# Narrower unread matmuls at the start, and seven output stores issued in halves, in an attention and mixer kernel

## The chip, the cores and the metric

The kernel runs on one core of one Trainium2 chip. The metric is the device time of one execution in microseconds (us). It was measured in three runs: 286.3, 287.03 and 287.74, a median of 287.03 us. A profile of one further execution was taken; its span, from the first to the last instruction, is 285.6 us.

The core has a matmul engine (PE, with its weight loads listed apart as PEld), a vector engine (DVE), an activation engine (ACT), a general engine (POOL) and a sequencer for transfers (SP). Each runs its own list of instructions in order and waits on semaphores for the others. Transfers (DMAs) are issued by SP, by ACT or by POOL and run on 16 DMA engines.

## The reference

Causal attention in blocks of 64 over 8 batches, 8 heads, 576 positions and 64 elements a head, followed by a mixer: one product over the positions, with a residual, and one over the channels, with a residual.

```python
def _attn_ref(q, k, v):
    scores = scale * np.matmul(q, k.transpose(0, 1, 3, 2))
    mask = block_i >= block_j            # blocks of 64 positions
    scores = np.where(mask, scores, -1000000000.0)
    scores = scores - np.max(scores, axis=-1, keepdims=True)
    attn = np.exp(scores)
    attn = attn / (np.sum(attn, axis=-1, keepdims=True) + 1e-09)
    return np.matmul(attn, v)

def _moe_ref(x, w_tok1, w_tok2, w_ch1, w_ch2):
    xt = x.transpose(0, 2, 1)
    h = np.maximum(xt @ w_tok1, 0.0) @ w_tok2
    u = x + h.transpose(0, 2, 1)
    h2 = np.maximum(u @ w_ch1, 0.0) @ w_ch2
    return u + h2
```

The output is float32, 8 x 576 x 512.

## The kernel before

The program is written as a list of operations. Each has the engines that may run it, the operations it depends on, and a function `emit` that issues its instructions. The text `ORDER` names all operations in the order in which they are emitted, each with the engine that runs it and the PSUM banks that it takes; so the order on every engine is fixed by hand, and a change inside one `emit` leaves the order of the operations as it is.

The batches are worked one after another, and pieces of neighbouring batches are interleaved on PE. For a batch, q and k are loaded and transposed on DVE (L442); PE makes scores of 64-row blocks (L566), ACT takes the exponentials (L585 for batch 0, L772 for most of the others), PE multiplies by v (L616, L669), and DVE divides by the sums. Then the mixer follows: the product over positions (L807 and L902), a transpose of the result `u_sb` to `uT` on PE for the early batches (L989) and by a DMA of SP from batch 2 on (L969, and L979 for the last 64 positions of two batches together, `um_sb`), the first channel product (L1030, L1103, L1227) and the second (L1361). DVE folds the second product's parts into `o_sb` (L1407), and SP stores `o_sb` to HBM (L1450 for the first 512 positions, L1436 for the rest).

Two places matter here.

The first is the start. `raise_clock` issues matmuls whose results nobody reads: their operands are a tile of zeros, `zeros`, which lies in `wd_sb`, and their output goes to a PSUM bank that is handed back at once. One operation at the very start of PE issues `WARM` = 11 of them with 512 columns (L371). Then there are 110 operations of one matmul with 256 columns each (L378), of which `ORDER` takes 37: 13 directly behind the first block, and 24 in groups of one to nine between the score matmuls of batch 0, up to 17.4 us. Each matmul is issued with its own load of 128 x 128 weights. The first score matmul waits for a transpose of q that waits for a load.

The second is the store of the output at the end of `channel_down_fast`. `o_sb` is a ring of three buffers, each of 128 x 2 x 512 float32, and a batch takes two of them, `row` 0 and `row` 1. For batches 0 to 6 both tiles of a row are finished together (`joint`), so a row is stored by one transfer of 512 KB on SP. Batch 7 is done in two turns of one tile each, in smaller transfers. SP's list also holds the transposes and the first loads of k and q. A buffer of `o_sb` may be written again when its store has landed.

Of the kernel before, what the change touches and what calls it, by code (L numbers as in the profile page):

```python
# [182 lines left out]
def kernel(  # L183
# [11 lines left out]
    nc = tc.nc  # L195
# [15 lines left out]
    def ring(n, shape, dtype, name, pool=sb):  # L211
        return [pool.tile(shape, dtype, name=f"{name}{i}", uniquify=False) for i in range(n)]
# [35 lines left out]
    o_sb = ring(3, [128, 2, DM], FP32, "o_sb")  # L248
# [13 lines left out]
    zeros = wd_sb[:, 0, 0:2, :].rearrange("p c s -> p (c s)")  # L262
# [16 lines left out]
    WARM, KEEP = 11, 110  # L279
# [25 lines left out]
    def bank_of(note):  # L305
        if note["pool"] in EARLY:
            return mm[note["slot"]]
        if not late:
            held_banks[0].__exit__(None, None, None)
            held_banks[0] = tc.tile_pool(name="singles", bufs=1, space=bass.MemoryType.PSUM)  # L310
            late.extend(ring(4, [128, 512], FP32, "late", held_banks[0].__enter__()))
        return late[note["slot"]]
# [8 lines left out]
    def reads(key, op):  # L321
        readers.setdefault(key, []).append(op)
        return op
# [41 lines left out]
    def raise_clock():  # L365

        bank = {"covers": True}

        def emit(o, bank=bank):
            for _ in range(WARM):  # L370
                nc.tensor.matmul(out=bank_of(bank), lhsT=zeros[:, 0:128], rhs=zeros, start=True, stop=True)  # L371

        P.add("PE", WARM * 0.427, emit, pads["zeros"], -1e6, take=[(BANK, bank)], give=[bank], at=1.2)
        for n in range(KEEP):
            bank = {"covers": False}

            def emit(o, bank=bank):
                nc.tensor.matmul(  # L378
                    out=bank_of(bank)[:, 0:256], lhsT=zeros[:, 0:128], rhs=zeros[:, 0:256],
                    start=True, stop=True,  # L380
                )

            P.add(
                "PE", 0.11, emit, pads["zeros"], 1e6, take=[(BANK, bank)], give=[bank], at=5.0 + 0.12 * n, until=20.0,
                quick=True,
            )
# [930 lines left out]
    def channel_down_fast(b, g_done, wc2_ready, u_done, prio):  # L1317
# [4 lines left out]
        oi, si = [], []  # L1322
# [9 lines left out]
        for ts in ((0, 1),) if joint else ((0,), (1,)):  # L1332
            c0, nt = ts[0], len(ts)
# [5 lines left out]
            for n, (dst, x, y, op) in enumerate(  # L1339
                ((s1, a21, a22, ADD), (s2, s1, a11, SUB), (s4, a12, s2, SUB), (a21, a11, a21, SUB))  # L1340
            ):
                def emit(o, dst=dst, x=x, y=y, op=op):
                    nc.vector.tensor_tensor(out=dst, in0=x, in1=y, op=op)

                war = s_war[n] if n < 3 else []
                made.append(P.add(
                    "DVE", dve_cost(768 * nt, 2), emit, g_done + war + made[-1:], prio - 2 + 0.1 * c0 + 0.01 * n,
                ))
                reads(g_key(b), made[-1])
# [3 lines left out]
            def product(n, to, x, y, made=None, s=None, c0=c0, nt=nt, banks=banks, last=last):  # L1353
                bank, first = banks[to], n in (0, 1)

                def emit(o, n=n):
                    if n == 0:
                        cover(banks["c"])
                    for i in range(nt):
                        for kk in range(H6):  # L1360
                            nc.tensor.matmul(  # L1361
                                out=bank_of(bank)[:, 256 * i : 256 * i + 256],
                                lhsT=x[:, kk, 128 * i : 128 * i + 128], rhs=y[:, kk],
                                start=first and i == 0 and kk == 0, stop=kk == H6 - 1,
                                skip_group_check=not first or i > 0,
                            )

                op = last[to] = P.add(
                    "PE", mm_cost(256, H6 * nt), emit, g_done + wc2_ready + wd_ready + [last.get(to), made],
                    prio + 0.005 * c0 + 0.02 * n,  # L1370
                    take=[(SEED, banks["c"]), (BANK, bank)] if n == 0 else [(BANK, bank)] if first else (),
                )
                reads(g_key(b), op)
                if s is not None:
                    reads(("s", si[s]), op)
                return op

            def turn(row, col):
                bank = {"covers": True}

                def emit(o):
                    for i in range(4):
                        nc.tensor.matmul(
                            out=bank_of(bank)[:, 128 * i : 128 * i + 128],
                            lhsT=uT[0][:, 2 * row + i // 2, 2 * col + i % 2, :], rhs=ident,
                            start=i == 0, stop=True, skip_group_check=i > 0,
                        )

                op = P.add("PE", mm_cost(128, 4), emit, u_done, prio - 0.5, take=[(BANK, bank)])
                reads(("uT", 0), op)  # L1390

                def emit(o):
                    cast(
                        o, ut[:, 2 * row : 2 * row + 2, 256 * col : 256 * col + 256],
                        bank_of(bank).rearrange("p (t c) -> p t c", c=256),
                    )

                return P.add(EVAC, evac_cost(512), emit, [op], prio - 0.5, give=[bank])
# [47 lines left out]
            rows = out[b, 0:512, :].rearrange("(r t p) d -> r p t d", r=2, t=2)  # L1446
            pieces = [(0, 0, 2), (1, 0, 2)] if c0 == 0 else [(0, 0, 2), (1, 1, 2), (1, 0, 1)]
            for row, h0, h1 in pieces:
                def emit(o, row=row, cols=slice(256 * h0, 256 * h1), c0=c0, nt=nt):
                    (nc.scalar if o.engine == "ACT" else nc.sync).dma_start(  # L1450
                        out=rows[row][:, c0 : c0 + nt, cols], in_=o_sb[oi[row]][:, c0 : c0 + nt, cols]
                    )

                op = P.add(
                    ("SP", "ACT") if b == B - 1 else "SP", 0.5, emit, [folded[row, h] for h in range(h0, h1)], prio, xfer=4 * 0.086 * nt * (h1 - h0)
                )
                reads(("o", oi[row]), op)
# [102 lines left out]
```

## Time and profile before

| | |
|---|---|
| median of 3 runs | 287.03 us (286.3 to 287.74) |
| profiled execution: span | 285.6 us |
| profiled execution: time | not listed |
| PE busy | 273.9 us, 96% of the span |
| DVE busy | 239.2 us, 84% |
| ACT busy | 179.4 us, 63% |
| POOL busy | 72.6 us, 25% |
| transfers | 31.96 MB, 112 GB/s on average |
| stores of 512 KB (L1450, SP) | 14, 3.2 us median to landing |

The profile's page gives busy time and the number of instructions of each engine, transfer queues, the chain of work that ended last, and the costliest groups of instructions. Rows of the chain have start, length and what ran. Rows of the timeline have start, length, engine, line, operation, output and input, and a count; neighbours of one form are merged, so the start of such a row is that of its first instruction, and its length reaches to the end of its last. In square brackets stands the idle time before it and what ended that. Rows of waits have who waited for whom, the sum in us, how often, and the longest. Rows of windows have the stretch, its length, and the busy time of PE, PEld, DVE, ACT and POOL with the count of instructions in brackets, then the granted clock, the share of the DMA engines and GB/s. A row for one line has its count, the shortest, the median and the longest duration in ns, and the first and the last start. Rows of queues have the packets, MB and the share of the DMA engines' time; the queue of kind "instruction" carries program code.

### The profile page before, as it was taken

How to read it: one execution, taken by the hardware profiler on the slowest of the kernel's cores; microseconds unless marked ns; L12 is line 12 of the kernel's file. 1: busy time of each engine (PE TensorE's matmuls, PEld its weight loads, DVE VectorE, ACT ScalarE, POOL GpSimd, SP SyncE). 2: the span in 40 equal slices, each digit the busy share in tenths (PEclk: the TensorE clock that was granted, in tenths of full speed). 3: DMA queues.
4: the chain of work that ended last, by engine and by line, in shares of the span. 5: the costliest groups of instructions: out<-in, count | busy, mean ns of one | idle time of the engine just before them, and what ended most of it. 6: DMA issues, size and time to landing. Idle time of an engine off the chain costs nothing.

```text
span 285.6 us, 9485 instructions
## 1 busy us (share of the span) xinstructions
PE 273.9 (96%) x4047; PEld 200.5 (70%) x4068; DVE 239.2 (84%) x515; ACT 179.4 (63%) x331; POOL 72.6 (25%) x126
## 2 busy tenths in 40 slices
PE   7899999999997999999999999999999999999992
PEld 3467565599675788986877668744589876578882
DVE  3588769999888898999998979769896995689982
ACT  3798888945996856897879865364524745642100
POOL 8895861502540351063332210000000000000000
PEclk9999999999999999999999999999999999999998
DMA  7999999936979492999598595101056301200255
GB/s 170 168 164 195 200 193 200 182 50 145 97 109 103 75 154 54 174 184 168 68 116 136 79 175 50 75 0 21 0 108 122 142 0 73 76 2 2 98 156 188
DMA packets 64778, 31.96 MB, mean 112 GB/s; under 512 B 53088, under 2 KB 55776, under 8 KB 64736
## 3 DMA queue, kind: packets, MB, share of 16 engines
q0 software_dynamic: 44896, 17.49, 53.0%
q1 hardware_dynamic: 19408, 13.21, 20.3%
q8 instruction: 32, 0.52, 0.7%
q10 hardware_dynamic: 432, 0.66, 0.7%
q14 instruction: 10, 0.08, 0.1%
HBM read 35.85 MB, written 9.44 MB: 159 GB/s over the span
## 4 chain that ended last, share of the span: by engine, by line
PE 90%; ACT 4%; DMA 1%; issue 1%; POOL 1%; DVE 0%; POOLq 0%
PE late L1361 23%; PE mm L1103 8%; PE mm L1227 7%; PE mm L566 7%; PE mm L1361 7%; PE late L1227 6%; PE late L1103 6%; PE mm L616 5%; PE mm L807 3%; PE late L616 2%; ACT e_sb L585 2%; PE mm L902 2%; PE late L566 2%; PE late L1030 2%; PE mm L1030 2%; PE late L807 2%
## 5 line engine op out<-in xcount | busy, mean ns | idle before, releaser
L772 ACT ACTIVATE e_sb<-mm 128x512 bf16<-128x512 f32 x82 | 46.6, 607 | 12.7 <-PE late L566 9.0
L772 ACT ACTIVATE e_sb<-late 128x512 bf16<-128x512 f32 x86 | 48.5, 610 | 9.2 <-PE late L566 8.4
L442 DVE STREAM_TRANSPOSE qk_sb<-qk_sb 128x288 int32<-128x288 int32 (+1 forms) x65 | 41.7, 695 | 3.4 <-PE sc L566 1.4
L468 POOL DMA_DIRECT2D vals<-in_v_dram x45 | 36.9, 829 | 5.9 <-PE mm L616 2.4
L1361 PEld LDWEIGHTS <-gT 128*128 128x128 bf16 x336 | 32.0, 98 | 5.6 <-issue 0.4
L1361 PEld LDWEIGHTS <-sums 128*128 128x128 bf16 x324 | 31.3, 98 | 5.2 <-issue 0.4
L566 PEld LDWEIGHTS <-qk_sb 32*64 32x64 bf16 x1280 | 19.6, 104 | 14.4 <-issue 10.7
L566 PE MATMUL mm<-qk_sb 32*64 32x512 bf16 (+7 forms) x560 | 27.4, 289 | 0.4
L616 PEld LDWEIGHTS <-e_sb 128*128 128x128 bf16 x640 | 23.3, 97 | 6.2 <-issue 3.6
L566 PE MATMUL late<-qk_sb 32*64 32x512 bf16 (+7 forms) x560 | 26.4, 294 | 0.3 <-ACT e_sb L585 0.3
L1361 PE MATMUL late<-wd_sb,gT 128*128 128x256 bf16 x168 | 20.7, 273 | 0.0
L1361 PE MATMUL late<-wd_sb,sums 128*128 128x256 bf16 x168 | 20.6, 273 | 0.0
L1103 PEld LDWEIGHTS <-ws_sb 128*128 128x128 bf16 x192 | 18.2, 98 | 3.0 <-issue 0.9
L642 DVE TENSOR_TENSOR x_sb<-mm,rinv 128x256 bf16<-128x256 f32 x45 | 18.7, 422 | 1.3
L616 PE MATMUL mm<-vals,e_sb 128*128 128x65 bf16 x450 | 19.7, 193 | 0.0
L1407 DVE TENSOR_TENSOR o_sb<-late,u_sb 128x512 f32<-128x512 f32 x22 | 15.0, 685 | 3.6 <-PE late L1361 3.6
L1361 PE MATMUL late<-wc_sb,gT 128*128 128x256 bf16 x132 | 16.2, 273 | 0.1
L1103 PEld LDWEIGHTS <-wc_sb 128*128 128x128 bf16 x144 | 15.3, 114 | 1.4 <-issue 0.4
L1227 PEld LDWEIGHTS <-ws_sb 128*128 128x128 bf16 x96 | 9.3, 98 | 9.8 <-issue 0.2
L594 POOL COPY vals<-e_sb 128x256 bf16<-128x256 bf16 (+1 forms) x11 | 4.3, 394 | 39.4 <-ACT e_sb L772 39.2
L400 ACT COPY mm<-late 128x512 f32<-128x512 f32 (+1 forms) x16 | 9.2, 572 | 8.1 <-PE late L1227 5.3
L793 ACT ACTIVATE gT<-mm 128x512 bf16<-128x512 f32 x21 | 12.6, 619 | 1.9 <-PE mm L1103 0.9
(198 smaller groups left out, 625.7 us busy)
## 6 DMA issues: line engine op xcount, KB each, us to landing
out_dram<-o_sb SPq DMA_DIRECT2D x14, 512.0 KB, 3.2
qk_sb<-in_k_dram POOLq DMA_DIRECT2D x14, 288.0 KB, 6.3
qk_sb<-in_q_dram POOLq DMA_DIRECT2D x14, 288.0 KB, 5.8
vals<-in_v_dram POOLq DMA_DIRECT2D x28, 128.0 KB, 4.5
wc_sb<-in_moe_w_ch_dram POOLq DMA_DIRECT2D x8, 192.0 KB, 7.7
wc_sb<-in_moe_w_ch_dram POOLq DMA_DIRECT2D x3, 512.0 KB, 10.4
out_dram<-o_sb SPq DMA_DIRECT2D x5, 256.0 KB, 3.3
vals<-in_v_dram POOLq DMA_DIRECT2D x15, 64.0 KB, 5.1
```

The lines of the kernel that those rows point to most:

```text
L442: nc.vector.transpose(dst[:, 0:S, :] .rearrange("p s e -> p (s e)") .bitcast(I32) .rearrange("p (a k) -> p k a", k=NB)[:, k0:k1], raw2.bit ...
L468: nc.gpsimd.dma_start(out=t[128 - p : 128, J, hs, 0:64], in_=src)
L566: nc.tensor.matmul(out=home(n)[64 * half : 64 * half + 64, c : c + w], lhsT=bar[r, 0] if j is None else kT[i][r, 64 * j : 64 * j + 64, par ...
L616: nc.tensor.matmul(out=u[:, I, 0:65], lhsT=e[:, h, c : c + 128], rhs=vt[:, J, head, 0:65], start=(J == 0), stop=(J == I),)
L642: nc.vector.tensor_tensor(out=xt[:, 0:4, 64 * head : 64 * head + 64], in0=u[:, :, 0:64], in1=ri[:, 0:4].to_broadcast([128, 4, 64]), op=MULT,)
L772: nc.scalar.activation(dst, bank_of(x), EXP, scale=scale)
L793: nc.scalar.activation(dst, src, RELU)
L807: nc.tensor.matmul(out=ps, lhsT=w1_sb[:, c, tt : tt + 255 : 2], rhs=xt[:, c, cols], start=(c == 0), stop=False)
L1103: nc.tensor.matmul(out=bank_of(bank)[:, 256 * o_ : 256 * o_ + 256], lhsT=x(o_, m), rhs=y[:, :, m, :], start=opens, stop=m == 1, skip_group ...
L1227: nc.tensor.matmul(out=bank_of(bank), lhsT=x(m), rhs=y[:, :, m, :], start=first and m == 0, stop=m == 1, skip_group_check=not first,)
L1361: nc.tensor.matmul(out=bank_of(bank)[:, 256 * i : 256 * i + 256], lhsT=x[:, kk, 128 * i : 128 * i + 128], rhs=y[:, kk], start=first and i ...
L1407: nc.vector.tensor_tensor(out=dst, in0=src, in1=other, op=ADD)
```

## The change

`raise_clock` issues 40 matmuls of 128 columns and one of 512 in place of 11 of 512: 5,632 columns in both. Each matmul of 256 columns (L378) becomes two of 128 in the same bank. The store of `row` 0 in batches 0 to 6 becomes two transfers, one for each tile of 128 rows; `row` 1 is stored as before. In batch 7 `nt` is 1, so nothing changes there, and the stores of the last 64 positions (L1436) are untouched.

PE's program grows by 134 instructions (67 loads and 67 matmuls, all of them up to 17.4 us in the old timeline), SP's by seven transfers. DVE, ACT and POOL have the same operations in the same order. The semaphores that SP's and ACT's transfers take in turn (eight of them) are dealt out anew behind the first split store, and where an operation waits for a store of a whole row 0 it now waits for two transfers.

```diff
         def emit(o, bank=bank):
-            for _ in range(WARM):
-                nc.tensor.matmul(out=bank_of(bank), lhsT=zeros[:, 0:128], rhs=zeros, start=True, stop=True)
+            for n in range(4 * WARM - 3):
+                w = 128 if n < 4 * WARM - 4 else 512
+                nc.tensor.matmul(
+                    out=bank_of(bank)[:, 0:w], lhsT=zeros[:, 0:128], rhs=zeros[:, 0:w], start=True, stop=True,
+                )
...
             def emit(o, bank=bank):
-                nc.tensor.matmul(
-                    out=bank_of(bank)[:, 0:256], lhsT=zeros[:, 0:128], rhs=zeros[:, 0:256],
-                    start=True, stop=True,
-                )
+                for i in range(2):
+                    nc.tensor.matmul(
+                        out=bank_of(bank)[:, 128 * i : 128 * i + 128], lhsT=zeros[:, 0:128], rhs=zeros[:, 0:128],
+                        start=True, stop=True,
+                    )
...
                 def emit(o, row=row, cols=slice(256 * h0, 256 * h1), c0=c0, nt=nt):
-                    (nc.scalar if o.engine == "ACT" else nc.sync).dma_start(
-                        out=rows[row][:, c0 : c0 + nt, cols], in_=o_sb[oi[row]][:, c0 : c0 + nt, cols]
-                    )
+                    step = 1 if row == 0 else nt
+                    for t0 in range(c0, c0 + nt, step):
+                        (nc.scalar if o.engine == "ACT" else nc.sync).dma_start(
+                            out=rows[row][:, t0 : t0 + step, cols], in_=o_sb[oi[row]][:, t0 : t0 + step, cols]
+                        )
```

## The prediction

> **What bounds the kernel now.** I read the page's busy shares first, then the chain that ended last, then the waits of the matmul engine.
>
> ```profile
> PE 273.9 (96%) x4047; PEld 200.5 (70%) x4068; DVE 239.2 (84%) x515; ACT 179.4 (63%) x331; POOL 72.6 (25%) x126
> PE 90%; ACT 4%; DMA 1%; issue 1%; POOL 1%; DVE 0%; POOLq 0%
> PE sc L566 <- DVE qk_sb L442: 1.8, 1, 1.8
> PE late L616 <- issue: 1.4, 1, 1.4
> PE mm L371 <- DVE wd_sb L344: 1.2, 1, 1.2
> PE late L566 <- ACT e_sb L585: 0.3, 1, 0.3
> ```
>
> PE is busy 96% of the span and is 90% of the chain. Its four listed waits come to 4.7 us: 1.2 before the first unread matmul, 1.8 after the first block of them, 0.3 behind an exponential, and 1.4 with no releaser that the profile shows ("issue"). Whatever is added to PE after the first block is paid in full, unless it fits into one of these; whatever is added before it has 1.8 us of room. No PE wait names a store.
>
> The stretch that the first edit touches is the start:
>
> ```profile
> 3.68 4.20 DMA qk_sb<-in_q_dram
> ...
> 7.89 0.43 DVE qk_sb L442
> ...
> 8.37 0.74 PE sc L566 x27
> ```
>
> This is the chain in order of time. The first scores at 8.37 wait for a load that lands at 7.88 and its transpose, not for PE.
>
> **Edit one, the unread matmuls.** The timeline of PE at the start:
>
> ```profile
> 1.20 3.91 PE L371 MATMUL mm<-wd_sb 128*128 128x512 bf16 x11 [1.20 <-DVE wd_sb L344]
> 4.95 1.58 PE L378 MATMUL mm<-wd_sb 128*128 128x256 bf16 x13
> 8.37 0.51 PE L566 MATMUL sc<-qk_sb 32*64 32x192 bf16 x28 [1.83 <-DVE qk_sb L442]
> ...
> 9.03 1.16 PE L378 MATMUL mm<-wd_sb 128*128 128x256 bf16 x9
> ```
>
> and, in small windows, two neighbours early and two late, with the start in the first column:
>
> ```profile
> 1.60 1.06 PE L371 MATMUL mm<-wd_sb 128*128 128x512 bf16 x2
> 2.03 1.06 PE L371 MATMUL mm<-wd_sb 128*128 128x512 bf16 x2
> ...
> 4.09 0.59 PE L371 MATMUL mm<-wd_sb 128*128 128x512 bf16 x2
> 4.30 0.59 PE L371 MATMUL mm<-wd_sb 128*128 128x512 bf16 x2
> ```
>
> Early starts are 0.43 us apart, late ones 0.21: the clock doubles near 4.0. The block of L371 had 11 matmuls of 512 columns; now it has 40 of 128 and one of 512, so 30 more matmuls and 30 more weight loads. The 37 matmuls of L378 that run become 74, each half as wide: 37 more pairs. Price of a narrow pair at the full clock:
>
> ```profile
> 64.91 0.61 PE L989 MATMUL late<-ident,u_sb 128*128 128x128 bf16 x8
> 65.36 0.27 PE L1361 MATMUL late<-wd_sb,gT 128*128 128x256 bf16 x1
> ```
>
> Eight 128-wide matmuls, each with its own 128x128 load, hold PE from 64.91 to 65.36: 0.056 us a pair, so the load is hidden there. At the half clock no row shows such pairs. The lower bound is a quarter of 0.427, 0.107. The upper adds the whole weight load of that stage, 0.147:
>
> ```profile
> L371 PEld LDWEIGHTS <-wd_sb x11: 97/147/147, 1.2 to 4.5; 128*128 128x128 bf16 x11
> ```
>
> that is 0.254. I take 0.107, because the nearest row (L989) shows loads overlapped. Sum: from 1.20 to 4.01 come 26 pairs; 14 more at 0.056 are 0.78, the wide one 0.21, so the block ends its issue at 5.0 (before: 4.95). The 13 matmuls of L378 become 26 at 0.056, 1.46 (before: 13 at 0.109, 1.42). PE is idle from about 6.6 instead of 6.53; the first scores still start at 8.37. Cost nothing, hidden by the load. If no load overlapped at either clock (0.254, then 0.056 + 0.097), 11 pairs fit before 4.01, 29 more take 4.5, the 26 take 4.0 and the start slips to about 12.8, 4.4 us: that is the far end.
>
> The Trainium skill, "TensorE: Matmul & The Clock Gate", section "Back-to-back issue gap", says that a stream of load and matmul pairs sustains only about 81 ns a matmul at 128 columns. By that figure the 74 would cost 2 us more than the 37 did; the 0.056 of L989 disagrees, and the sum stays with the row.
>
> After 8.37 there are 24 old matmuls of L378 (37 less 13), so 48 narrow ones, each pair of them 2 x 0.056 less 0.109 = 0.003 longer: 0.07 us. ACT covers part of it:
>
> ```profile
> 9.13 12.16 ACT L585 ACTIVATE e_sb<-sc 128x384 bf16<-128x384 f32 x14 [2.33 <-PE sc L566]
> ```
>
> It is busy without a break from 9.13 to 21.29. I charge the 0.07 in full.
>
> **Edit two, the stores.** Seven stores of 512 KB become fourteen of 256 KB: seven more issues on SP, the same bytes. Behind four of the split stores SP has a transpose or nothing; its own timeline:
>
> ```profile
> 65.53 0.41 SPq L1450 DMA_DIRECT2D out_dram<-o_sb  x1
> 87.31 5.29 SPq L969 DMA_TRANSPOSE uT<-u_sb  x2
> ...
> 118.16 2.10 SPq L1450 DMA_DIRECT2D out_dram<-o_sb  x2
> 123.87 1.20 SPq L979 DMA_TRANSPOSE umT<-um_sb  x1
> 151.11 0.37 SPq L1450 DMA_DIRECT2D out_dram<-o_sb  x1
> 161.14 1.24 SPq L969 DMA_TRANSPOSE uT<-u_sb  x1
> ...
> 183.04 0.37 SPq L1450 DMA_DIRECT2D out_dram<-o_sb  x1
> 196.13 1.20 SPq L979 DMA_TRANSPOSE umT<-um_sb  x1
> ...
> 218.92 51.43 SPq L1450 DMA_DIRECT2D out_dram<-o_sb  x7
> 271.71 4.85 SPq L1436 DMA_DIRECT2D out_dram<-o_sb  x3
> ```
>
> An issue takes 0.4 us. Its far end is the 118.16 pair, 2.10 for two, so at most 1.7 for one. The splits stand at 65.53, second at 118.16, at 151.11, at 183.04, and three among the seven from 218.92. The tightest gap to a transpose is 120.26 to 123.87, 3.6 us, wider than 1.7. The last store of that form ends at 270.35 with 1.4 to spare, and it is not split. Cost 0. If the cover at 120 were gone, one transpose would be late by up to 1.7. The semaphores that SP's transfers take in turn shift by seven, so a transfer now waits for one that is nearer in time; by program order the closest pair is the last store of all behind the first L1436 transfer, which went out at 271.71 and has four further transfers of SP between; I charge nothing. A buffer is released when both halves have landed, 0.4 to 1.7 later; DVE's list of waits names no store at all.
>
> **What moves with the instruction count.** The one unexplained PE wait:
>
> ```profile
> q8 instruction: 32, 0.52, 0.7%
> ...
> 90.04 1.40 issue
> ...
> q8 instruction: 1, 0.02, 5.5%
> ```
>
> The first row is of the page's queues, the second of the chain, the third of the queues between 89.0 and 90.1. 0.52 MB in 32 packets for the 8115 PE instructions of the first fence is 64 bytes each and 256 to a packet. The one packet near the stop starts in that window; a window from 79.2 to 89.0 has none. The stop falls after instruction 3,263 of PE's program order, which is 12 packets of 256 and 191. I read it, as an inference, as PE running out of fetched code: the packet came late while loads and transposes filled the DMA engines, and PE resumed 2.4 us after it began. The change puts 134 instructions (67 pairs) ahead of everything later, so every such border moves back by 134 old instructions. Counted in program order, the border met at 91.44 is met at 87.44 instead. What counts is how fast PE runs through the 256 between two borders. Stretches of the old trace:
>
> ```profile
> 16.86:21.62 4.76, 4.40 (x136) 2.71 (x128) 3.59 (x16) 4.76 (x6) 4.45 (x8) 1.00 1.39 153
> 83.98:89.85 5.87, 5.58 (x140) 3.98 (x138) 5.45 (x17) 5.34 (x11) 1.10 (x2) 1.00 1.65 159
> 41.07:44.35 3.28, 3.28 (x134) 2.85 (x131) 2.81 (x14) 2.06 (x5) 0.89 (x1) 1.00 1.09 216
> 24.46:29.11 4.65, 4.60 (x134) 3.85 (x130) 4.50 (x13) 2.73 (x7) 2.08 (x4) 1.00 1.14 206
> 118.15:122.95 4.80, 4.80 (x148) 4.02 (x125) 4.63 (x15) 3.97 (x8) 0.40 (x1) 1.00 1.28 247
> 151.55:155.41 3.86, 3.86 (x130) 3.11 (x129) 3.23 (x9) 3.34 (x8) 1.10 (x2) 1.00 1.10 191
> ```
>
> The first two are stretches of the old cut, and the second is the one that stopped; the other four are of the new cut. Old cut: three stretches under 5.0 us (the shortest 4.76) and one stop in 31. New cut: seven under 5.0, two of them under 4. From entry to resumption the stopped one took 5.87 + 1.40 = 7.27; the 4.76 one did not stop. The 3.28 one follows a slow stretch (29.11 to 41.07) in which its request may go out early; I leave it out. A stop in the 3.86 stretch costs between 0 and 3.4, in the 4.65 one up to 2.6, in the 4.80 one up to 2.5. I take stops of 1.9 in all, one as seen and a part of a second, nearer to the row that stopped than to none: net of the 1.40 that goes, +0.5.
>
> The Trainium skill, "Runtime: NRT & Kernel Launch", section "Instruction fetch mechanics", says the sequencer refills in 16 KiB blocks of 256 instructions and that the cost of a border is mostly hidden. The size agrees with the 32 packets; by "hidden" the +0.5 would be 0, but then the 1.40 has no cause.
>
> **Sum.** 0 + 0.07 + 0 + 0.5 on this execution's span of 285.6 gives 286.2. The execution's own time is not listed; its span lies 1.4 below the median of 287.03, so the forecast is 287.6.
>
> **The rivals.**
> Slower: code fetch decides. Place: the stretches that the old trace runs at 24.5 to 29.1, 118.2 to 123.0 and 151.6 to 155.4, all amid DMA traffic of 191 to 247 GB/s. It decides where a packet lands later than the stretch's 3.9 to 4.8 us; one stop at the full 3.4 less the 1.40 is +2.0, a second of 2.0 to 2.5 makes it +4.0 to +4.5: 289.1 to 291.6. Against it: the 4.76 stretch passed at 153 GB/s.
> Faster: the stop at 90.04 is gone and no other comes: -1.40 + 0.07, 285.7. For it: 30 of 31 old stretches did not stop; against it, the new ones are shorter.
> The clock: narrow matmuls with gaps raise it later. If it came a whole 3.4 us later (7.4), 40 x 0.107 + 0.43 end at 5.9, 26 x 0.107 at 8.7: +0.3 to +0.5, 288. If it stayed low through the 9 to 21 stretch, up to +8.
> That the change does not do what it says can be left out: the program order of the changed kernel has all 67 added pairs and seven added stores.
>
> **How the numbers follow.** About 0.5%, 1.4 us, is what a measurement here can tell from no change. Forecast (stops about as before or a little longer, -0.3 to +1.3): 0.43, all within the bound. Code fetch slower: 0.33. Stop gone: 0.20; its 285.7 lies just inside the bound at 285.6, so I count 0.13 of it as faster and 0.07 as within. Clock or serial loads: 0.04, slower. So faster 0.13, within 0.50, slower 0.37. The range, 285.5 to 290.3, takes in the stop gone and most of the slower case; the forecast's own is 286.7 to 288.4.
>
> **What would show it.** PE's first block still ends before 7, and L566 starts at 8.4 (serial loads: near 12). The issue wait at 90.04 is gone from its place, and any new one lies at a border of 256 instructions, with a q8 packet beginning about 2.4 us before it resumes. SP's transposes keep their starts relative to PE. I am wrong if PE waits for DVE or DMA grow behind a store, or if the time differs with PE's idle unchanged.

## The result and the profile after

The changed kernel took 289.89 us (median of 22 executions, 286.68 to 293.70) against 287.26 us for the kernel before (22 executions, 286.2 to 290.33). The ratio is 1.0067, 95% interval 1.0042 to 1.0093, so about 1.9 us slower. It leaves out the executions that took over 1.5% more than the shortest of their kernel (four of the changed kernel's 22); over all of them the medians differ by 2.6 us. The profiled execution of the changed kernel took 288.02 us, with a span of 286.2.

The page of the changed kernel, and its waits of PE (who waited for whom, us in total, times, longest):

```profile
PE 276.1 (96%) x4135; PEld 204.2 (71%) x4135; DVE 239.1 (84%) x515; ACT 179.6 (63%) x331; POOL 72.3 (25%) x126
q8 instruction: 32, 0.52, 0.7%
```

```profile
PE mm L620 <- DVE qk_sb L446: 1.9, 1, 1.9
PE mm L372 <- DVE wd_sb L344: 1.2, 1, 1.2
PE mm L815 <- issue: 1.1, 1, 1.1
PE sc L570 <- DVE qk_sb L446: 1.0, 1, 1.0
PE mm L620 <- DMA vals<-in_v_dram: 0.4, 1, 0.4
PE late L570 <- ACT e_sb L589: 0.3, 1, 0.3
PE mm L811 <- issue: 0.2, 1, 0.2
```

The 1.4 before L616 near 90 us is gone. In its place stand 1.1 before L815 and 1.9 before L620 (lines of the changed kernel are four higher here), and a small one of 0.2 before L811. PE's timeline around the two, and the transfer queues in the windows 28.45 to 29.6 and 45.5 to 46.6:

```profile
29.26 0.40 PE L811 MATMUL mm<-x_sb,w_sb 128*128 128x128 bf16 x4
30.79 0.19 PE L815 MATMUL mm<-x_sb,w_sb 128*128 128x64 bf16 x1 [1.13 <-issue]
...
45.59 0.60 PE L1034 MATMUL late<-uT,wc_sb 128*128 128x512 bf16 x2
48.06 0.46 PE L620 MATMUL mm<-vals,e_sb 128*128 128x65 bf16 x10 [1.87 <-DVE qk_sb L446]
```

```profile
DMA packets 167, 0.25 MB, mean 218 GB/s; under 512 B 18, under 2 KB 165, under 8 KB 165
...
q8 instruction: 1, 0.02, 5.2%
```

```profile
DMA packets 66, 0.25 MB, mean 227 GB/s; under 512 B 8, under 2 KB 8, under 8 KB 65
...
q8 instruction: 1, 0.02, 5.1%
```

In program order PE stopped ahead of instructions 1,215 and 1,727. Less 191 these are 4 and 6 times 256; the 0.2 before L811 falls at 959, which less 191 is 3 times 256. In both cases a code packet began shortly before (28.52 and 45.57 in the packet list), and PE went on 2.3 and 2.5 us later; in the kernel before it was 2.4. The second stop is put down to a DVE transpose that ended last; the next experiments show the same stop, at the same instruction, with no releaser.

The start of PE's timeline:

```profile
1.20 4.58 PE L372 MATMUL mm<-wd_sb 128*128 128x128 bf16 x41 [1.20 <-DVE wd_sb L344]
5.62 1.61 PE L382 MATMUL mm<-wd_sb 128*128 128x128 bf16 x26
8.22 0.51 PE L570 MATMUL sc<-qk_sb 32*64 32x192 bf16 x28 [0.98 <-DVE qk_sb L446]
```

The narrow block is over at 7.2 and PE still waits 0.98 us for the first scores.

The end. The last SP store of the kernel before and of the changed one, from its issue to its landing (last column, us):

```profile
out_dram<-o_sb SPq DMA_DIRECT2D x1, 128.0 KB, 3.4
```

```profile
out_dram<-o_sb SPq DMA_DIRECT2D x1, 128.0 KB, 2.1
```

The same 128 KB land 1.3 us sooner after the change. That gain was not forecast.

### The profile page after: what moved, and what is told of

Its sections match the earlier page's. It is cut to its first block, busy times and chain, and to the rows that moved or that the text cites. A ratio compares the mean times of both kernels' runs of the same rounds, so it can differ in the third digit from the quotient of the medians.

```text
span 286.2 us, 9653 instructions
## 1 busy us (share of the span) xinstructions
PE 276.1 (96%) x4135; PEld 204.2 (71%) x4135; DVE 239.1 (84%) x515; ACT 179.6 (63%) x331; POOL 72.3 (25%) x126
## 4 chain that ended last, share of the span: by engine, by line
PE 87%; DMA 6%; DVE 2%; issue 2%; ACT 1%; POOL 1%; SPq 0%; DVEq 0%
PE late L1365 23%; PE mm L1107 8%; PE mm L1231 7%; PE mm L1365 6%; PE mm L570 6%; PE late L1231 6%; PE late L1107 6%; PE mm L620 4%; PE mm L811 3%; DMA vals<-in_v_dram 3%; PE mm L906 2%; PE late L620 2%; PE late L906 2%; DMA qk_sb<-in_k_dram 2%; PE mm L1034 2%; PE late L811 2%
## 5 line engine op out<-in xcount | busy, mean ns | idle before, releaser
L620 PEld LDWEIGHTS <-e_sb 128*128 128x128 bf16 x640 | 23.1, 97 | 7.1 <-issue 4.3
L620 PE MATMUL mm<-vals,e_sb 128*128 128x65 bf16 x450 | 19.7, 193 | 2.4 <-DVE qk_sb L446 1.9
L797 ACT ACTIVATE gT<-late 128x512 bf16<-128x512 f32 x17 | 10.4, 612 | 6.6 <-PE late L1231 2.4
```

Of the source, the lines that this page charges most:

```text
L620: nc.tensor.matmul(out=u[:, I, 0:65], lhsT=e[:, h, c : c + 128], rhs=vt[:, J, head, 0:65], start=(J == 0), stop=(J == I),)
```

## The experiments

Two theories stood against each other. Code fetch: the change matters through PE's instruction count alone, which moves the borders of 256 at which PE can run out of code. Below, a border is named by its instruction, and a stop is a wait of PE at a border, with a code packet that began 2.2 to 2.5 us before PE went on. Its rivals: the widths of the unread matmuls, and the split stores.

**The kernel before, again.** No edit.

> The kernel before, unchanged, to see its own spread and granted clock run by run. Both theories: ratio 1.000 within 0.3%. Code fetch: one PE stop without a releaser near 90 us, 1 to 1.5 us. If the longer runs of the changed kernel (granted clock 0.993 and 0.987) come from its longer stops or its narrow matmuls, nearly all runs here have a clock of 0.997 or more; if the chip does that to any kernel, half of these runs have 0.994 or less too.

Ratio 1.0009 (0.9984 to 1.0033), span 284.4. This profile has no stop near 90 us, against the expectation, only a 0.3 without releaser near 28 us, at border 959:

```profile
PE sc L566 <- DVE qk_sb L442: 1.2, 1, 1.2
PE mm L371 <- DVE wd_sb L344: 1.2, 1, 1.2
PE mm L855 <- issue: 0.3, 1, 0.3
PE mm L566 <- DVE x_sb L642: 0.2, 1, 0.2
```

So the 1.4 in the first profile was one draw, not a fixture. All 12 executions had a granted clock of 0.995 or more; of the changed kernel's 22, twelve had 0.994 or less. This profile, without a stop of note, is the base of the differences below.

**The kernel before with 134 idle PE instructions.** Widths and stores as before; behind the thirteenth unread matmul:

```diff
+                for _ in range(67 if n == 12 else 0):
+                    nc.tensor.matmul(
+                        out=bank_of(bank)[:, 0:32], lhsT=zeros[:, 0:128], rhs=zeros[:, 0:32],
+                        start=True, stop=True,
+                    )
```

> The kernel before with all its widths and stores, and 67 pairs of a weight load and a 32-column matmul behind the first 13 unread matmuls of 256 columns: 134 PE instructions more, as in the changed kernel. The pairs take about 67 x 0.03 = 2.0 us of the 1.83 us in which PE waits, so the first scores start at 8.4 to 8.6. Code fetch: the stop near 90 us is gone, two stops without a releaser come near 29 and 44 to 48 us, 3 us or more together, and the time is 1.5 to 2.5 us above the kernel before, like the changed kernel (ratio 1.005 to 1.009). Widths or stores as the cause: the stop near 90 stays, ratio 1.000 to 1.002.

Ratio 1.0107 (1.0061 to 1.0153). PE's timeline:

```profile
29.11 0.40 PE L812 MATMUL mm<-x_sb,w_sb 128*128 128x128 bf16 x4
30.27 0.19 PE L816 MATMUL mm<-x_sb,w_sb 128*128 128x64 bf16 x1 [0.77 <-issue]
...
45.08 0.60 PE L1035 MATMUL late<-uT,wc_sb 128*128 128x512 bf16 x2
47.56 0.46 PE L621 MATMUL mm<-vals,e_sb 128*128 128x65 bf16 x10 [1.89 <-issue]
```

The same two instructions, 1,215 and 1,727, with waits of 0.77 and 1.89 against 1.13 and 1.87, and with every real matmul and store as in the kernel before. The first scores start at 8.60, which is 0.2 us later than in the kernel before. The wait of 1.89 has no releaser here, at the same instruction, which speaks against DVE as the cause of the 1.87 above. This is the decisive run: added instructions make the stops and the loss, with no width and no store changed.

**The split stores alone.** The third hunk of the change.

> Only the stores are split; PE's program is that of the kernel before. Code fetch: the same single stop near 90 us, ratio 1.000 within 0.3%. Stores as the cause: ratio 1.004 to 1.009 and PE or DVE waits that name a transfer of SP.

Ratio 1.0006 (0.998 to 1.0033), span 284.4, as for the kernel before, and no wait names a store. The stop near 90 us did not come here either.

**Both matmul splits, stores whole.** The first two hunks.

> Both splits of the unread matmuls, the stores whole. Code fetch: the stops of the changed kernel, near 29 and 45 to 48 us, none near 90, ratio 1.004 to 1.009. Stores as the cause: ratio 1.000 to 1.002. It does not tell the widths from the count of instructions; that is for the padded kernel beside it.

Ratio 1.0103 (1.0067 to 1.0138). Its two longest stops precede instructions 1,215 and 1,727 once more:

```profile
32.67 0.19 PE L815 MATMUL mm<-x_sb,w_sb 128*128 128x64 bf16 x1 [1.40 <-issue]
...
49.98 0.46 PE L620 MATMUL mm<-vals,e_sb 128*128 128x65 bf16 x10 [1.90 <-issue]
```

Two more waits of this profile fall at borders, 1.1 us at 703 and 0.4 at 959. They are put down to ACT and DVE, but here too a code packet began 2.2 us before PE went on. This kernel and the padded one have the same count and differ in the widths, and their ratios, 1.0103 and 1.0107, are the same within their intervals; so the widths add nothing that shows.

**The first block alone.** The first hunk; 60 instructions more.

> Only the first block is split (40 of 128 columns and one of 512); 60 PE instructions more, so every border of 256 falls at a place of its own. Code fetch: no stop at the places of the changed kernel (before the 64-column matmul of L811 near 29 us, before the first L616 near 45 us) and none at that of the kernel before (90 us); a stop only at an instruction whose number is 191 and a multiple of 256, ratio 0.997 to 1.007. Widths: the first scores or the clock come later, ratio 1.004 or more with PE waits that fetch borders do not explain.

Ratio 1.0033 (1.0010 to 1.0056). Two stops, at borders 1,727 and 3,263 of its own count:

```profile
PE mm L672 <- issue: 1.6, 1, 1.6
...
PE mm L619 <- issue: 0.9, 1, 0.9
```

The expectation named 45 and 90 us as places without a stop, and one came close to each (from 46.8 and from 90.4), but before other instructions (in the middle of a group of L619, and in L672). The rule of the borders held; the forecast of which borders stop did not.

**The unread matmuls joined.** The reverse of the change: neighbours of 256 columns become one of 512, 32 instructions fewer.

```diff
-                nc.tensor.matmul(
-                    out=bank_of(bank)[:, 0:256], lhsT=zeros[:, 0:128], rhs=zeros[:, 0:256],
-                    start=True, stop=True,
-                )
+                place = [n - k for k in (0, 13, 22, 26, 29, 33, 36) if n >= k][-1]
+                last = n in (12, 21, 28, 35, 36)
+                w = 256 if last else 512
+                if last or place % 2 == 0:
+                    nc.tensor.matmul(
+                        out=bank_of(bank)[:, 0:w], lhsT=zeros[:, 0:128], rhs=zeros[:, 0:w],
+                        start=True, stop=True,
+                    )
```

> The reverse of the change: neighbouring unread matmuls of 256 columns are joined to 512, same columns in all, 16 pairs or 32 PE instructions fewer than before; stores as before. Code fetch: the last border (instruction 8,127 of 8,138) is not reached any more, so no code packet runs beside the last stores, and the time from PE's last matmul to the end of the span is 1.0 to 1.3 us shorter than in the kernel before; ratio 0.994 to 0.998 if no new stop comes in mid-program, and none at the places of the changed kernel. Widths as the cause: 0.998 to 1.000, the end as before.

Ratio 0.9930 (0.9911 to 0.9949), a median of 284.49 us, the fastest kernel of this study, and below the range that was expected. No wait of note falls at a border, and the end is short, as expected:

```profile
PE mm L371 <- DVE wd_sb L344: 1.2, 1, 1.2
PE sc L570 <- DVE qk_sb L446: 0.9, 1, 0.9
PE mm L620 <- DMA vals<-in_v_dram: 0.6, 1, 0.6
PE mm L620 <- DVE e_sb L603: 0.4, 1, 0.4
PE late L570 <- ACT e_sb L589: 0.3, 1, 0.3
PE mm L382 <- issue: 0.2, 1, 0.2
```

```profile
out_dram<-o_sb SPq DMA_DIRECT2D x1, 128.0 KB, 2.1
```

The end can be compared over all twelve profiles, as the time from PE's last matmul start to the end of the span. The kernels with a border a few instructions ahead of PE's end (the kernel before twice, the split stores alone, and the aligned kernel below) show 5.50, 5.22, 5.25 and 5.28 us; their last code packet begins between 0.4 us before and 2.0 us after that last start. The other eight show 3.80 to 4.26, and their last packet lies 4.7 us or more earlier. The last store takes 3.1 to 3.5 us to land in the first four and 2.0 to 2.1 in the others. So the changed kernel is spared about 1.2 us at the end because its last border moved away from the last stores. In the joined kernel the end accounts for about half of the 2.0 us that it gains; where the rest comes from stays open.

**The changed kernel, aligned.** 61 idle pairs more in the changed kernel, so that its count is 256 above the kernel before (the edit is that of the padded kernel with 61 for 67).

> The changed kernel with 61 pairs of a weight load and a 32-column matmul more behind the first 13 groups of unread matmuls, 256 PE instructions more than before in all, so every border falls where it does in the kernel before. The pairs take about 1.9 us where PE has 1.0 us of room, so the first scores start up to 0.9 us later. Code fetch: no stop near 30 and 46 us, the end as in the kernel before, ratio 1.000 to 1.004 (the later start). Widths or stores: ratio 1.007 or more, as the changed kernel and the late start on top.

A miss: 1.0075 (1.0032 to 1.0118). The ratio rests on two executions (287.71 and 290.12 us); the other six took 292.2 to 294.5, with granted clocks of 0.970 to 0.974, the lowest of the study, and none of these was profiled. The profile shows stops where it should have had none:

```profile
PE sc L575 <- issue: 1.5, 1, 1.5
PE mm L864 <- issue: 1.3, 1, 1.3
```

The first comes at 13.2 us, at border 447: the 61 pairs hold 122 instructions in 1.7 us, so PE reached that border in the scores of batch 0. The second is the border at which the kernel before waits 0.3; here the wait is 1.3. The first scores started at 9.56, later than expected. This kernel does not tell the widths from the count; equal borders did not give equal stops. A kernel with the narrow widths and the old count was not run.

**The changed kernel, again.** No edit.

> The changed kernel, unchanged, for another profile. Code fetch: the stops near 30 and 46 us again at the same two instructions, about 1 and 2 us. If the runs with a granted clock of 0.993 come from a clock that falls for one window of 3.41 us after the longer stop, a profile of such a run shows a stretch of 0.5 that begins at 46 to 50 us.

Ratio 1.0090 (1.0049 to 1.0131). The profiled execution had a granted clock of 0.988 and a span of 289.7, so it can show what the longer executions are made of. Windows of 3.41 us: stretch, length, busy us (instructions) of PE, PEld, DVE, ACT, POOL, then the granted clock, DMA share, GB/s:

```profile
23.20:26.61 3.41, 1.70 (x44) 1.55 (x43) 2.72 (x11) 1.97 (x5) 1.48 (x4) 1.00 1.03 181
26.61:30.02 3.41, 3.41 (x60) 2.94 (x59) 1.28 (x3) 1.13 (x3) 1.69 (x4) 0.50 1.14 204
30.02:33.43 3.41, 3.30 (x83) 2.69 (x83) 2.75 (x8) 2.15 (x5) 1.61 (x2) 1.00 1.16 208
47.09:50.50 3.41, 1.51 (x36) 0.98 (x25) 1.84 (x6) 2.06 (x4) 0.00 (x0) 1.00 1.06 212
50.50:53.91 3.41, 3.41 (x32) 1.23 (x31) 2.02 (x6) 1.53 (x3) 0.00 (x0) 0.50 1.89 141
53.91:57.32 3.41, 3.36 (x39) 1.62 (x39) 3.28 (x8) 2.96 (x7) 1.60 (x3) 1.00 0.05 3
```

Twice a window in which PE was busy half of the time or less is followed by one at half clock. The second has the stop at 1,727 inside it (48.0 to 49.9). The first has a stop from 25.0 to 26.5 at border 959; the stop at 1,215 that was expected did not come. Against the kernel before, PE's lag at the same matmuls grows from 1.87 to 3.36 us over the first slow window and from 4.94 to 6.48 over the second, 1.5 us each. One such window in a span of 286 us makes a mean granted clock of 0.994, and two make 0.988, which is this profile's. The values near 0.993 and 0.987 of other executions fit one and two such windows, but none of these was profiled.

A low share of PE alone does not bring the slow window. The first profile of the changed kernel and that of the first block alone have a window as empty, on the same grid of 3.41 us counted from the moment at which the full clock came, and the next one is at full clock:

```profile
46.31:49.72 3.41, 1.66 (x30) 0.80 (x29) 1.88 (x6) 1.54 (x4) 0.00 (x0) 1.00 1.17 202
49.72:53.13 3.41, 3.41 (x60) 1.64 (x46) 3.23 (x10) 3.33 (x7) 0.69 (x2) 1.00 1.66 117
...
88.74:92.15 3.41, 1.62 (x43) 0.80 (x43) 1.86 (x6) 3.38 (x7) 0.00 (x0) 1.00 1.79 103
92.15:95.56 3.41, 3.41 (x96) 2.89 (x95) 2.15 (x8) 1.11 (x3) 0.00 (x0) 1.00 0.64 123
```

What decides between them is open.

**The unread matmuls of 256 columns alone.** The second hunk; 74 instructions more.

> Only the 37 matmuls of 256 columns are split into 74 of 128; 74 PE instructions more, a third placing of the borders. Code fetch: instruction 1,727 then falls in the second group of L616 near 46 us, which PE reaches sooner after the border before it than at any other border of this placing, so one stop of about 1 us there, as the kernel with only the first block split has; the last border lies well ahead of the end, so the end is 1.0 to 1.3 us shorter than before; ratio 0.998 to 1.005. Widths: ratio 1.005 or more without such a stop.

Half a hit. There is a stop at 1,727, of 0.7 us, at the place that the count gave in advance, and the end is short (4.23). But three other borders stop too, 959, 1,215 and 3,263, and the ratio is 1.0066 (1.0038 to 1.0094), above the range:

```profile
PE late L567 <- issue: 2.5, 2, 1.7
...
PE mm L617 <- issue: 0.7, 1, 0.7
PE mm L670 <- issue: 0.7, 1, 0.7
```

**Joined matmuls and split stores.** The joined kernel with the third hunk.

> The unread matmuls joined to 512 columns (32 PE instructions fewer) and the stores split as in the change. Code fetch: as the kernel with the joined matmuls alone, ratio 0.991 to 0.996, no stop, the end short. Stores as a part of the cause: 0.996 or more, with waits that name a transfer of SP.

Ratio 0.9949 (0.9929 to 0.9969), within the range, and its interval overlaps that of the joined kernel alone. One wait, however, names a store, in DVE's list, and PE waits for DVE there:

```profile
DVE o_sb L1411 <- DMA out_dram<-o_sb: 1.1, 1, 1.1
```

```profile
PE late L1365 <- DVE o_sb L1411: 0.7, 1, 0.7
```

A fold at 268.6 waits for an `o_sb` buffer; PE's lag against the kernel before grows from 0.38 to 1.24 us there. The two halves of batch 6's row went out on SP at 263.8 and 264.2, and a code packet began at 265.5. The joined kernel alone, whose packet came at 266.1, has no such wait. The second half landed 4.4 us after its issue. In the first profile of the changed kernel and in that of the stores alone, where no code packet began while it was under way, the same half landed after 2.3. That points at the packet beside it; the two were not tried apart.

## Why the prediction was right, and where it was not

Outcome: slower by 0.67%, within the range, and in the case "code fetch decides", which had 0.33; the likeliest case, within 0.5%, did not come. The mechanism was right: new stops, at borders of 256 with a late code packet. That the time fell in the range is in part luck: the stops were sized too small, a gain at the end was missed, and the two errors, +1.4 and -1.2, nearly cancel. So even the forecast span of 286.2 was met, while the median, forecast at 287.6, came 2.3 us higher. Of the steps:

- **The unread matmuls cost nothing at the start: right.** The narrow pairs at half clock stood 0.107 us apart (starts at 2.78 and 2.88), as taken. The block ended at 5.62 and not at 5.0, because the full clock came at 5.35 in this execution and not at 4.0; it came anywhere from 4.0 to 7.2 in the profiles of this study. PE had 0.98 us left.
- **The figure of 81 ns a matmul** (the Trainium skill, "TensorE: Matmul & The Clock Gate", section "Back-to-back issue gap") does not fit: the 26 matmuls of L382 take 1.61 us, 62 ns each with the last one's full length counted in, and its starts are 56 ns apart.
- **The stores are hidden: right for this change.** SP's pairs took 0.8 us, no wait of the changed kernel names a store, and the stores alone gave 1.0006. In the joined kernel the cover was gone once, for 0.86 us of PE. The prediction charged nothing for a buffer that is released later; that term is zero only while the fold comes later still.
- **The borders move by 134: right**, and the padded kernel shows it as the cause. The stretch from 24.46 to 29.11 was named, and the stop at 1,215 is its end. That the stop at 90 goes was forecast too, but it proves little, as the next profile of the kernel before has none there either.
- **Where it failed: the size of the stops, 1.9 in all.** I left out the stretch from 41.07 to 44.35 because its request could go out early. It holds the larger stop, 1.9 us (2.0 of lag), in all four profiles of kernels with 134 instructions more. The request did not go out early: PE passed the border before it at 42.7 in the changed kernel, and the packet began at 45.57. The stretches at 118 and 152 us, on which the slower rival was priced, did not stop, so the slower case came at one of its three places only. With the stop at 1,215, 1.3 us, the sum is 3.3.
- **The net of the 1.40 that goes.** That stop is not in two later profiles of kernels with the same PE program. On average less than 1.40 went.
- **Two terms were missing.** At the end 1.2 us are gained. And the clock can fall for one window or two after a stop, at about 1.5 us each; twelve of the 22 executions of the changed kernel have a granted clock that fits this. The rival of the clock spoke only of the start.

Against the second profile of the kernel before the account closes: +1.3 at instruction 1,215, +2.0 at 1,727, -0.3 from an earlier start and small shifts between, -1.2 at the end, 1.8 in all; the spans are 286.2 and 284.4. The fallen clock comes on top in other executions.

The Trainium skill, "Runtime: NRT & Kernel Launch", section "Instruction fetch mechanics", calls the cost of a block border mostly hidden. The runs here agree for most of the 32 borders, and differ at none to four of them a profile, by 0.2 to 1.9 us each. How fast PE runs through a block does not decide it alone. In the first profile of the changed kernel, the block ahead of border 1,727 stopped, and one almost as fast, ahead of border 5,823, did not:

```profile
42.74:46.19 3.45, 3.45 (x134) 2.85 (x131) 2.97 (x14) 2.23 (x5) 0.38 (x1) 1.00 1.07 217
153.66:157.52 3.86, 3.86 (x130) 3.10 (x129) 3.23 (x9) 3.34 (x8) 1.10 (x2) 1.00 1.00 178
```

The code packet of the first began at 45.57, 0.6 us before PE needed it; that of the second at 153.94, 3.6 us before. That packets are late because of other transfers is an inference: loads fill the DMA queues at the stops (218 and 227 GB/s in the two windows of the result), but no run took these loads away.

## What to carry to other kernels

An edit that leaves PE's work alone but changes its number of instructions moves every fetch border behind it; compare it with a kernel that has the same count and no edit before judging the edit. A PE wait without a releaser, or with an implausible one, that falls at a border of 256 (here 191 and a multiple of it) with a code packet begun some 2.3 us before is likely a fetch stop. Which borders stop could not be forecast here, so a kernel with the new count has to be run. Here taking 32 unread instructions away was worth 0.7%.

## What the runs showed that was not expected

A code packet beside the last stores lengthens the end of the program by 1.2 us (5.2 to 5.5 against 3.8 to 4.3). A stop of 1.5 or 1.9 us can be paid twice, when the next window of 3.41 us runs at half clock (after PE was busy 1.70 and 1.51 us of a window; after 1.66 and 1.62 in two other profiles it did not). The kernels with 134 instructions more had a granted clock of 0.994 or less in 22 of 40 executions, the two joined kernels in none of 15, and the kernel before in one of the 61 that were run beside the experiments.
